# Reordering how three engines build the transform tables at the start of a spectral filter with a GEGLU branch

## The chip, the cores and the metric

The kernel runs on one core of a Trainium2 chip. The metric is the device time of one execution in microseconds (us), here the median of three runs. Profiles come from the hardware profiler and cover one execution each.

## What is computed

A sequence of 2048 rows of width 640 is normalised row by row (xn). One branch takes the real 2-D Fourier transform of xn, multiplies it by complex weights and transforms back. The other is a GEGLU feed-forward net (FFN) on the same xn, with a silu behind it. The product is added to the input.

```python
S, D, F = 2048, 640, 1536
def _A_ref(x, w_r, w_i):                 # spectral branch
    X = jnp.fft.rfft2(x.astype(jnp.float32), axes=(-2, -1))
    X = X * (w_r + 1j * w_i)
    return jnp.fft.irfft2(X, s=(S, D), axes=(-2, -1)).astype(jnp.bfloat16)
def _B_ref(x, w_gate, w_up, w_down):     # FFN branch
    return (_gelu(x @ w_gate) * (x @ w_up)) @ w_down
x = A_x
xn = _layernorm(x, axis=-1)
s = _A_ref(xn, A_w_r, A_w_i)
g = _silu(_B_ref(xn, B_w_gate, B_w_up, B_w_down))
return x + s * g
```

## The kernel before

**Tiling.** The 2048 rows are 16 slabs of 128 rows; slab n1 holds the rows n1, n1+16, n1+32 and so on. Four slabs make a group of the FFN. The transforms are matmuls with tables of sines and cosines that the kernel makes itself: along the rows in two steps (128 points by Tinv and Tfwd, 16 points by MG, N1 and N2), along the width by FT (forward) and FI (inverse).

**Engines.** TensorE (PE) runs all matmuls and transposes. ScalarE (ACT) applies gelu, silu and Sin and copies results out of PSUM. VectorE (DVE) does the row statistics, most of the normalising, the gating product uT, and elementwise work of the spectral branch. GpSimd (POOL) does the roots of the variances and the integer and float phases of the tables. SyncE (SP) issues all DMAs, in one queue. Every engine runs its own instructions strictly in the order in which the program issues them.

**The order** is written out by hand. The list `back` holds 144 pieces of FFN work, called places here: places 0 to 2 are FFN pieces of slabs 0 and 1 with the normalising of slabs 1 to 3; places 3 to 7 are the tiles t = 3 to 7 of the columns of slabs 0 and 1; places 8 to 15 the tiles 0 to 7 of the columns of slabs 2 and 3; places 16 to 23 the tiles 8 to 11 of the whole group 0, psg (gate) and psu (up) in turn; places 24 to 35 the down projection of group 0. Three more groups follow, of 24 pieces and 12 down pieces each. `put(s, f, ...)` lets f be issued right behind place s, in the order of the put lines. Each gate piece issues five matmuls into a bank psg and then a gelu on ACT (L669); each up piece five matmuls into a bank psu and then the product uT on DVE (L671). There are two banks of each kind, so a piece waits until the piece two before it of its kind has been read.

**The tables.** Each of the five columns of the forward table FT starts as an ACT instruction `ft_v` (L328): index times a scale plus a bias, both per partition, from the list `ab`. Three POOL instructions (`ft_phase`, L333, L335, L337) reduce the phases, and `ft_sin` on ACT takes the Sin. Steps 0 to 4 belong to FT, 5 to 9 to FI. Tinv comes from POOL phases (`tinv_phase`, L303), a mask on DVE (`tinv_mask`, L308) in two halves, and a Sin on ACT (L315); `tfwd` transposes it to Tfwd. The 16-point table comes from `mg_iota`, `mg_phase1` and `mg_phase2` (POOL: 2, 11 and 8 small instructions), `mg_mask` (DVE), `mg_sin` (ACT) and `mg_build` (POOL). The scales and biases in `ab` are small DVE constants of one column: `fwd_consts` makes those of the forward table, `inv_consts` those of the inverse table.

**Normalising.** `stats(n1)` takes mean and variance of a slab on DVE. `root(n0, n)` adds eps on DVE (ve, L188) and raises to the power -1/2 on POOL (rst, L190) for n slabs at once. Slabs 0 to 3 have their roots one by one and are normalised on DVE (`norm`, `norm_parts`, L196). Slabs 4 to 7 have one root of four columns and a `shift` (POOL: nm, then nmr, L424), and ACT normalises them (`norm_act`, L429) in places 15, 17, 19 and 21. Their transposes for FFN group 1 are DMA transposes (`slab_T(..., 2)`, L460), put in places 17 to 23 and issued by SP behind the loads that stand ahead of them in its queue. `fold_a` and `fold_b` (DVE) prepare pairs of normalised slabs for the spectral branch; `slab_S1` (PE, then Z on ACT, L478) and `pair_D` (pd) carry them through the first two transforms, and the results go through DRAM (ZDR) to the next stage, `pair_S2` (px).

**Around the change.** Ahead of place 0 the program issues `fwd_consts`, the first half of an iota, stats(0), root(0, 1), `inv_consts`, then warm-up matmuls, norm of slab 0, stats(1), slab 0's transposes, two more warm-ups and root(1, 1).

Of the kernel before, what the change touches and what calls it, by code (L numbers as in the profile page):

```python
# [31 lines left out]
def kernel(  # L32
# [40 lines left out]
    with tc.manual_schedule():  # L73
        build(nc, locals())


def build(nc, env):
# [79 lines left out]
    def c1(name, dt=FP32):  # L157
        return consts.tile([P, 1], dt, name=name)
# [26 lines left out]
    def root(n0, n):  # L185
        m = mva[n0 // 4][:, n0 % 4:n0 % 4 + n, :]
        ve = work.tile([P, 4], FP32, tag="ve", name="ve")[:, 0:n]
        nc.vector.tensor_scalar(out=ve, in0=m[:, :, 1], scalar1=1e-5, scalar2=None, op0=ALU.add)  # L188
        r = work.tile([P, 4], FP32, tag="rst", bufs=4, name="rst")[:, 0:n]
        nc.gpsimd.tensor_tensor(out=r, in0=ve, in1=mhalf[:, 0:n], op=ALU.pow)  # L190
        rall[n0] = r
        for k in range(n):
            rstd[n0 + k] = r[:, k:k + 1]
# [29 lines left out]
    def bits(name, fields):  # L223
        n = len(fields)
        ti = consts.tile([P, n], INT32, name=name + "i")
        tf = consts.tile([P, n], FP32, name=name)
        for k, (shift, mask) in enumerate(fields):
            nc.vector.tensor_scalar(out=ti[:, k:k + 1], in0=pint, scalar1=shift, scalar2=mask,
                                    op0=ALU.logical_shift_right, op1=ALU.bitwise_and)
        nc.vector.tensor_copy(out=tf, in_=ti)  # L230
        return [tf[:, k:k + 1] for k in range(n)]

    def affine(name, src, a, b):
        t = c1(name)
        nc.vector.tensor_scalar(out=t, in0=src, scalar1=float(a), scalar2=float(b), op0=ALU.mult, op1=ALU.add)
        return t

    u_f, hi_f, s_f, h_f, pf, n1_f, z_f = bits(
        "pb", [(0, 63), (6, 1), (0, 31), (5, 1), (0, 127), (1, 15), (0, 1)])
# [4 lines left out]
    def fma(name, src, k, add, dt=FP32):  # L244
        t = c1(name, dt)
        nc.vector.scalar_tensor_tensor(out=t, in0=src, scalar=float(k), in1=add, op0=ALU.mult, op1=ALU.add)
        return t
# [8 lines left out]
    def times(name, src, k, by):  # L256
        t = c1(name)
        nc.vector.scalar_tensor_tensor(out=t, in0=src, scalar=k, in1=by, op0=ALU.mult, op1=ALU.mult)
        return t
# [6 lines left out]
    ab = []  # L266
    kc = []
# [10 lines left out]
        ab.extend([(a_m, b_0), (a_m, b_1), (a_m, b_2), (a_m, b_3), (a_r, b_r)])  # L278

    def inv_consts():  # L280
        cq = kc[0]
        i_0 = affine("i_0", pf, 4.0, 0.0)
        i_1 = affine("i_1", pf, 4.0, 4.0)
        i_2 = affine("i_2", pf, 4.0, 2.0)
        o_0 = affine("o_0", pf, 2.0, 320.0)
        o_1 = affine("o_1", pf, 2.0, 2.0)
        o_2 = affine("o_2", pf, 2.0, 321.0)
        o_3 = affine("o_3", pf, 2.0, 1.0)
        l_k = fma("l_k", h_f, 2.0, affine("l_s", s_f, 2.0, 256.0))
        l_r = fma("l_r", times("lh", affine("hk", h_f, -2.0, 1.0), 1.0, hi_f), 1.0, l_k)  # L290
        i_r = affine("i_r", l_r, 2.0, 0.0)
        o_r = fma("o_r", l_r, 1.0, cq)
        ab.extend([(i_0, o_0), (i_1, o_1), (i_2, o_2), (i_2, o_3), (i_r, o_r)])

    fwd_consts()
    vt_iota(0)
    stats(0)
    root(0, 1)
    inv_consts()

    def tinv_phase(h):
# [201 lines left out]
    def warm_pe(n):  # L503
        if not warm_bank:
            warm_bank.append(bank(0))
        for _ in range(n):
            nc.tensor.matmul(warm_bank[0][:, 0:256], lhsT=ones[:, 0:P], rhs=ones, start=True, stop=True)
# [238 lines left out]
    def put(s, *item):  # L746
        plan[s].append(item)
# [2 lines left out]
    put(5, slab_T, 2, 1)  # L750
    put(6, slab_T, 3, 0)
    for g in range(5):
        put(7 + g, ft_v, g)
        put(12 + g, ft_v, 5 + g)
    put(7, tinv_phase, 0)
    put(7, tinv_phase, 1)
    put(9, mg_iota)
    put(9, mg_phase1)
    for k in range(3):
        put(11, ft_phase, 0, k)  # L760
    for k in range(4):
        put(7 + 2 * k, stats, 4 + k)
    put(13, root, 4, 4)
    put(13, shift, 4, 4)
    put(13, mg_phase2)
    for k in range(3):
        put(16, ft_phase, 1, k)
    put(14, tinv_mask, 0)
    put(15, tinv_mask, 1)
    for k in range(4):  # L770
        put(15 + 2 * k, norm_act, 4 + k)
        put(17 + 2 * k, slab_T, 4 + k, 2)
# [3 lines left out]
    for it in ((silu_table,), (tinv_sin,), (ft_sin, 0)):  # L776
        put(23, *it)
    put(24, fold_b, 0)
    put(25, mg_mask)
    put(25, root, 8, 2)  # L780
    put(25, mg_sin)
    put(25, mg_build)
    put(25, fold_a, 1)
    put(26, tfwd, 0)
    put(27, tfwd, 1)
# [1 line left out]
    put(28, fold_b, 1)  # L787
    put(29, stats, 10)
    put(29, ft_sin, 1)
    put(31, norm, 9)  # L790
    put(32, stats, 11)
    put(33, root, 10, 2)
# [59 lines left out]
    slab_Tparts(0)  # L852
    warm_pe(2)
    root(1, 1)

    put(5, phase_const)

# [35 lines left out]
```

## Time and profile before

| | us |
|---|---|
| median of three runs | 209.15 |
| lowest, highest | 209.08, 209.93 |
| profiled execution | 209.03 |
| its span, first to last instruction | 207.3 |
| PE busy | 198.6 (96%) |
| DVE busy | 132.2 (64%) |
| ACT busy | 124.6 (60%) |
| POOL busy | 34.5 (17%) |

The granted clock of PE was 0.999 of full speed over the span. The page of the profile cuts the span into 40 slices of 5.2 us and gives the busy share of each in tenths (9 is 90% or more):

```profile
PE   7799997999999999999999999999999999999993
POOL 5327799592001100000000000000000000000000
```

PE is below 90% in the first two slices, in the sixth (26 to 31 us) and in the last. POOL has nearly all its work in the first nine slices.

In the chain of waits, each piece of time belongs to the engine that the end of the program waited for at that moment. A timeline row gives start and length in us, engine, line, operation, written tile, read tiles, shapes, how many instructions the row merges, and in brackets the idle time ahead with what ended it. A row's length is from the start of its first instruction to the end of its last. Instructions of one engine overlap somewhat, so the next may start before the last has ended.

### The profile page before, as it was taken

What the parts mean: (1) busy time and instruction counts of PE and PEld (TensorE: products, weight loads), DVE (VectorE), ACT (ScalarE), POOL (GpSimd) and SP (SyncE); (2) the same over time, 40 slices, a digit from 0 to 9 for tenths busy, and PEclk for the clock granted to TensorE, in tenths of its full rate; (3) what the DMA queues carried; (4) which work ended last, traced back from release to release, by engine and by line L of the source; (5) the groups of instructions that cost most, each with busy time, mean ns of one, the idle gap of its engine ahead of it and who ended that gap; (6) DMA issues with size and microseconds to landing.
All of it is one profiled execution on the core that took longest, in us unless ns stands there. A gap on an engine that the chain in (4) does not pass through costs nothing.

```text
span 207.3 us, 4412 instructions
## 1 busy us (share of the span) xinstructions
PE 198.6 (96%) x1626; PEld 121.0 (58%) x1643; DVE 132.2 (64%) x357; ACT 124.6 (60%) x230; POOL 34.5 (17%) x61
## 2 busy tenths in 40 slices
PE   7799997999999999999999999999999999999993
PEld 5689853677655555465544444447775555556762
DVE  7787867896679762335555656424469678676653
ACT  2436729957887777425777777533555555656631
POOL 5327799592001100000000000000000000000000
PEclk9999999999999999999999999999999999999999
DMA  6999999999886999279964432349822332242111
GB/s 175 304 300 310 373 279 145 152 140 129 185 152 164 188 190 183 76 169 224 207 136 96 95 67 63 77 104 294 259 74 87 95 92 101 64 133 76 67 51 65
DMA packets 46200, 31.81 MB, mean 153 GB/s; under 512 B 12513, under 2 KB 43873, under 8 KB 46177
## 3 DMA queue, kind: packets, MB, share of 16 engines
q1 hardware_dynamic: 46176, 31.52, 67.3%
q8 instruction: 13, 0.21, 0.5%
q14 instruction: 11, 0.08, 0.2%
HBM read 21.66 MB, written 7.88 MB: 143 GB/s over the span
## 4 chain that ended last, share of the span: by engine, by line
PE 85%; DVE 5%; POOL 4%; issue 2%; ACT 1%; DMA 1%; DVEq 0%; ACTq 0%
PE psg L665 22%; PE psu L665 22%; PE psg L689 13%; PE psu L689 11%; PE pd L485 4%; PE pu L547 3%; PE pv L592 2%; PE pz L476 2%; PE pd L489 2%; PE px L527 2%; DVE st L174 2%; POOL GEN L335 1%; POOL rst L190 1%; DMA X<-in_A_x_dram 1%; POOL GEN L337 1%
## 5 line engine op out<-in xcount | busy, mean ns | idle before, releaser
L665 PE MATMUL psg<-xnT,Wg 128*128 128x512 bf16 (+2 forms) x284 | 59.9, 338 | 2.1 <-ACT ge L669 1.2
L665 PE MATMUL psu<-xnT,Wu 128*128 128x512 bf16 (+2 forms) x289 | 60.4, 339 | 0.6 <-issue 0.3
L671 DVE TENSOR_TENSOR uT<-psu,ge 128x512 bf16<-128x512 f32 (+2 forms) x59 | 34.4, 587 | 33.9 <-PE psu L665 27.3
L669 ACT ACTIVATE ge<-psg 128x512 bf16<-128x512 f32 (+2 forms) x59 | 30.5, 518 | 28.5 <-PE psg L665 27.3
L689 PEld LDWEIGHTS <-uT 128*128 128x128 bf16 x384 | 36.1, 98 | 15.2 <-issue 0.5
L665 PEld LDWEIGHTS <-Wu 128*128 128x128 bf16 x295 | 26.5, 98 | 21.8 <-issue 1.3
L665 PEld LDWEIGHTS <-Wg 128*128 128x128 bf16 x295 | 26.2, 98 | 22.1 <-issue 2.6
L689 PE MATMUL psg<-Wd,uT 128*128 128x320 bf16 (+1 forms) x192 | 30.4, 303 | 0.0
L689 PE MATMUL psu<-Wd,uT 128*128 128x320 bf16 (+1 forms) x192 | 29.6, 296 | 0.0
L534 DVE TENSOR_TENSOR p<-xs,W 128x642 bf16<-128x642 bf16 x32 | 14.4, 492 | 8.9 <-ACT xs L530 8.5
L497 ACT CAST zd<-pd 128x644 bf16<-128x644 f32 x15 | 12.3, 883 | 4.6 <-PE pd L489 4.6
L606 ACT ACTIVATE eo<-pd 128x640 bf16<-128x640 f32 x16 | 10.4, 701 | 7.4 <-PE pd L489 7.4
L594 ACT CAST vs<-pv 128x640 bf16<-128x640 f32 x16 | 11.0, 690 | 6.1 <-PE pv L592 6.1
L174 DVE BATCH_NORM_STATS2 st<-X 128x6 f32<-128x320 bf16 x32 | 14.1, 482 | 0.2 <-issue 0.2
L530 ACT CAST xs<-px 128x642 bf16<-128x642 f32 x16 | 11.1, 692 | 4.0 <-PE px L527 3.6
L190 POOL TENSOR_TENSOR rst<-ve,mhalf 128x1 f32<-128x1 f32 (+2 forms) x9 | 7.5, 831 | 30.4 <-DVE ve L188 30.4
L615 DVE TENSOR_TENSOR cs<-eo 128x640 bf16<-128x640 bf16 x16 | 7.1, 486 | 7.4 <-ACT eo L606 7.4
L478 ACT CAST Z<-pz 128x640 bf16<-128x640 f32 x16 | 11.0, 696 | 1.2 <-PE pz L476 1.2
L640 DVE TENSOR_TENSOR Yall<-Yall,G 128x640 bf16<-128x640 bf16 (+3 forms) x18 | 8.1, 450 | 1.8 <-ACT G L694 1.6
L698 DVE SCALAR_TENSOR_TENSOR G<-th,psg 128x320 bf16<-128x320 f32 x8 | 3.9, 486 | 7.6 <-ACT th L697 7.6
L641 DVE TENSOR_TENSOR Yall<-Yall,xt 128x640 bf16<-128x640 bf16 (+3 forms) x18 | 8.2, 455 | 0.6
L547 PE MATMUL pu<-p,N 64*64 64x321 bf16 x128 | 8.2, 304 | 0.1
(138 smaller groups left out, 214.8 us busy)
## 6 DMA issues: line engine op xcount, KB each, us to landing
ZDR<-zd SPq DMA_DIRECT2D x16, 160.5 KB, 4.1
UDR<-us SPq DMA_DIRECT2D x32, 80.2 KB, 2.5
xt<-in_A_x_dram SPq DMA_DIRECT2D x8, 320.0 KB, 3.1
W<-in_A_w_r_dram SPq DMA_DIRECT2D x14, 160.5 KB, 7.5
W<-in_A_w_i_dram SPq DMA_DIRECT2D x14, 160.5 KB, 5.0
out_dram<-Yall SPq DMA_DIRECT2D x14, 160.0 KB, 1.8
B<-ZDR SPq DMA_DIRECT2D x6, 321.0 KB, 8.2
Vin<-UDR SPq DMA_DIRECT2D x6, 321.0 KB, 5.5
```

Source lines behind the costliest of these rows:

```text
L174: nc.vector.bn_stats(out=st[:, k, :], in_=X[:, n1, 320 * k:320 * k + 320])
L478: nc.scalar.copy(out=Zt[n1], in_=pz)
L497: ev(out=zd.rearrange("p a c (m b) -> p a c m b", b=2)[:, :, :, :, b], in_=pd[b])
L530: nc.scalar.copy(out=xs.rearrange("p (k l) -> p k l", k=2), in_=px[:, :, 0:L])
L534: nc.vector.tensor_tensor(out=pp, in0=xs, in1=WT[:, h].rearrange("p k l -> p (k l)"), op=ALU.mult)
L547: nc.tensor.matmul(pu[64 * lo:64 * lo + 64, hh, 0:L], lhsT=NM[r, kind, 0:64], rhs=pp[r, lo * L:(lo + 1) * L], start=first, stop=not first)
L594: nc.scalar.copy(out=vs, in_=pv)
L606: nc.scalar.activation(out=eo[:, b], in_=py[b], func=ACT.Copy, scale=(2.0 if n0 // 4 in BY_SILU else 1.0) / (S * D))
L665: nc.tensor.matmul(ps, lhsT=WT[:, c, t * P:(t + 1) * P], rhs=xnT[g][:, c, c0:c1_], start=(c == 0), stop=(c == 4))
L669: nc.scalar.activation(out=ges[t], in_=ps, func=ACT.Gelu_apprx_tanh)
L671: nc.vector.tensor_tensor(out=uT[g][:, t, c0:c1_], in0=ps, in1=ges[t], op=ALU.mult)
L689: nc.tensor.matmul(ph, lhsT=uT[g][:, t, j * P:(j + 1) * P], rhs=Wd[:, t, c0:c1_], start=(t == 0), stop=(t == NT - 1))
```

## The change

Three things are edited, and no arithmetic is added or dropped.

- `inv_consts` is split. Seven constants of the first four inverse columns and the two that need only `s_f` and `h_f` (l_s, hk) stay where they were; the five others (l_k, lh, l_r, i_r, o_r) form `inv_rest`, issued behind root(1, 1).
- The ten ACT steps `ft_v` move from places 7 to 16 to places 3 to 12.
- On POOL, the forward phases (`ft_phase` 0) move from place 11 to 9, and the inverse phases (`ft_phase` 1) from place 16 to 13, behind root and shift of slabs 4 to 7. All phases of the 16-point table move behind those, in place 13; before, its iotas and first phases stood in place 9 and its second ones right behind the shift. On DVE the masks of Tinv move from places 14 and 15 to 12 and 14, and `mg_mask` from 25 to 28; `mg_sin` and `mg_build` move from place 25 to 29, behind `ft_sin` 1.

The queues of PE and SP issue the same instructions in the same order as before. On POOL the forward phases now follow the Tinv phases directly, then come the root of slabs 4 to 7, nm and nmr, the inverse phases and the 16-point phases. On ACT the steps come earlier among the gelus, with the copy of slab 2's transpose now directly ahead of the third step, and mg_sin comes behind the Sin of FI.

```diff
     def inv_consts():
-        cq = kc[0]
         i_0 = affine("i_0", pf, 4.0, 0.0)
...
         o_3 = affine("o_3", pf, 2.0, 1.0)
-        l_k = fma("l_k", h_f, 2.0, affine("l_s", s_f, 2.0, 256.0))
-        l_r = fma("l_r", times("lh", affine("hk", h_f, -2.0, 1.0), 1.0, hi_f), 1.0, l_k)
+        ab.extend([(i_0, o_0), (i_1, o_1), (i_2, o_2), (i_2, o_3)])
+        kc.append(affine("l_s", s_f, 2.0, 256.0))
+        kc.append(affine("hk", h_f, -2.0, 1.0))
+
+    def inv_rest():
+        cq, l_s, hk = kc
+        l_k = fma("l_k", h_f, 2.0, l_s)
+        l_r = fma("l_r", times("lh", hk, 1.0, hi_f), 1.0, l_k)
         i_r = affine("i_r", l_r, 2.0, 0.0)
         o_r = fma("o_r", l_r, 1.0, cq)
-        ab.extend([(i_0, o_0), (i_1, o_1), (i_2, o_2), (i_2, o_3), (i_r, o_r)])
+        ab.append((i_r, o_r))
...
     for g in range(5):
-        put(7 + g, ft_v, g)
-        put(12 + g, ft_v, 5 + g)
+        put(3 + g, ft_v, g)
+        put(8 + g, ft_v, 5 + g)
     put(7, tinv_phase, 0)
     put(7, tinv_phase, 1)
-    put(9, mg_iota)
-    put(9, mg_phase1)
     for k in range(3):
-        put(11, ft_phase, 0, k)
+        put(9, ft_phase, 0, k)
     for k in range(4):
         put(7 + 2 * k, stats, 4 + k)
     put(13, root, 4, 4)
     put(13, shift, 4, 4)
-    put(13, mg_phase2)
     for k in range(3):
-        put(16, ft_phase, 1, k)
-    put(14, tinv_mask, 0)
-    put(15, tinv_mask, 1)
+        put(13, ft_phase, 1, k)
+    for it in (mg_iota, mg_phase1, mg_phase2):
+        put(13, it)
+    put(12, tinv_mask, 0)
+    put(14, tinv_mask, 1)
...
-    put(25, mg_mask)
+    put(28, mg_mask)
     put(25, root, 8, 2)
-    put(25, mg_sin)
-    put(25, mg_build)
     put(25, fold_a, 1)
...
     put(29, ft_sin, 1)
+    put(29, mg_sin)
+    put(29, mg_build)
...
     root(1, 1)
+    inv_rest()
```

## The prediction

> **What bounds the kernel now.** I read the chain of waits first, over the whole span and then for its first 50 us; then the timelines of TensorE (PE), ScalarE (ACT), VectorE (DVE) and GpSimd (POOL) from 3 to 57 us; then the DMA issues that feed PE.
>
> ```profile
> PE 85%; DVE 5%; POOL 4%; issue 2%; ACT 1%; DMA 1%; DVEq 0%; ACTq 0%
> ```
>
> PE holds 85% of the chain. The rest is almost all ahead of 32.3 us, so only there can a change outside PE shorten anything. The chain of waits there (start, length, engine, written tile, line):
>
> ```profile
> 22.19 0.52 ACT GEN L328
> 22.79 0.88 POOL GEN L333
> 23.74 2.95 POOL GEN L335
> 26.76 2.14 POOL GEN L337
> 28.91 1.44 POOL rst L190
> ...
> 31.67 0.58 ACT ge L669
> 32.30 1.24 PE psg L665 x5
> ```
>
> POOL starts the forward table's phases when the fifth table step (L328) is done, needs some 6.1 us for them, and only then takes the root of slabs 4 to 7 (L190). The rows of PE and ACT show what that costs (start, length, operation, in brackets the idle time ahead of it):
>
> ```profile
> 29.86 1.24 PE L665 MATMUL psu<-xnT,Wu 128*128 128x512 bf16 x5
> 32.30 1.24 PE L665 MATMUL psg<-xnT,Wg 128*128 128x512 bf16 x5 [1.19 <-ACT ge L669]
> 30.84 0.92 ACT L429 ACTIVATE X<-X,nmr,rst 128x640 bf16<-128x640 bf16 x1 [3.77 <-POOL nmr L424]
> ```
>
> ACT stands in norm_act(4) until nmr comes at 30.8; the gelu of place 16 is behind it in ACT's queue, and its bank is what place 20 needs. Groups of five such matmuls follow each other 1.08 us apart, so place 20 was ready at 30.94 and started at 32.30: 1.36 us lost. The other stretch not set by PE is the start, on DVE and POOL:
>
> ```profile
> 4.93 0.16 DVE L246 SCALAR_TENSOR_TENSOR l_k<-pb,l_s 128x1 f32<-128x1 f32 x1
> ...
> 5.65 0.15 DVE L246 SCALAR_TENSOR_TENSOR o_r<-l_r,cq 128x1 f32<-128x1 f32 x1
> 5.71 0.63 DVE L196 TENSOR_SCALAR X<-X,mva,rst 128x384 bf16<-128x384 bf16 x2
> ...
> 8.25 0.64 DVE L196 TENSOR_SCALAR X<-X,mva,rst 128x384 bf16<-128x384 bf16 x2 [0.68 <-POOL rst L190]
> ```
>
> Slab 0's root was done at 5.08 (POOL row 4.50, 0.58 long), but its norm waited in DVE's queue behind the dependent constants until 5.71.
>
> **The change, part by part.** *Inverse constants split.* Eight constants and then hk stay ahead of norm(0); hk would issue near 4.81 instead of 5.01. Norm(0) then waits for the root alone: 5.08 plus the 0.03 that L196 took after the root at 8.22, so 5.11 against 5.71: 0.60 us earlier. Stats(1) follow at 5.65; their slab landed 3.9 us after its issue at 1.64, near 5.55, just in time. The five moved operations (l_k to o_r) stand behind ve of slab 1, where DVE idled 0.68 us for the root: with the spacings of before (0.07 for a free one, 0.19 to 0.20 for one that waits for the last) they take 6.88 to 7.48, and norm(1) is released by its root at 7.64. Cost nothing; without that cover 0.6. From there to place 5 the chain is DVE, POOL and PE work that moves along (the weights of places 3 to 7 land 1.4 us or more ahead of use). Bounds of this part: 0 (slab 1 late) to 0.60; I take 0.60, as every row on the way moves with it.
>
> *Forward table steps in places 3 to 7.* Ten ACT steps move four places earlier, none is added. At places 3, 4, 6, 7 and later they fill ACT's waits for PE (0.3 to 0.9 us; a step occupies the queue 0.42). At place 5 the step stands between the copy of slab 2's transpose and the gelu of place 6, which was back to back (15.63, 16.22): the gelu is 0.42 later, uT of place 6 some 0.28, as it waited for PE until 0.08 after the gelu, and so is the copy of slab 3's transpose (17.13 to 17.61) that place 8's matmul at 17.89 needs. Loss 0.05 us, between 0 and 0.3.
>
> *POOL's order.* All later times carry the 0.55 gained so far. POOL has the two phases of the 2048-point table (2.37 us) from 15.9 to 18.2, then the forward phases at once, since the fifth table step is done at 17.7: 0.87, 2.94 and 1.61 (L337's length the second time), with the 0.08 between them, to 23.8. The 4.5 us of the 16-point table's iotas, phase1 and phase2 on both sides of the root go behind it. On DVE, tinv_mask(0) now stands ahead of stats(7), in place 12. The two masks of before show what happens when one meets POOL:
>
> ```profile
> 26.63 0.81 DVE L308 TENSOR_SCALAR GEN<-GEN,andm,orm 128x1024 int32<-128x1024 int32 x1
> 27.68 1.77 DVE L308 TENSOR_SCALAR GEN<-GEN,andm,orm 128x1024 int32<-128x1024 int32 x1
> ```
>
> L337 ran from 26.76 to 28.90. The first mask started ahead of it and was free, and L337 took 2.14 instead of 1.61; the second started inside it, ended 0.55 after it, and took 0.96 more. So each waits for the other's end. In the new order mask 0 begins at 23.7, at L337's end, and waits 0.2 us at most; the uT of place 13 and stats(7) behind it run some 0.3 later than they would (24.71 and 25.05 before, less 0.55, plus 0.3), and ve ends near 26.1. The root of four columns took 1.48 with mask 1 inside it until 29.45, so 0.9 alone; 128x1 takes 0.56 and 128x2 alone 0.72 (row at 64.83), which extrapolates to 1.06. I take 1.06, up to 1.48: root 26.2 to 27.3. Mask 1, in place 14, starts inside the root and ends 0.55 after it, at 27.8; nm waits for that, nmr is ready at 28.3 (28.7 with the long root). Behind mask 1, uT of place 15 ends near 28.2, and the bank it frees is wanted by place 19 at 29.3. Free.
>
> Norm_act(4) starts at 28.3, the gelu of place 16 0.83 later, done at 29.7; place 20 wants its bank at 30.38. The stall is gone with 0.65 to spare: gain 1.36, between 0.7 (nmr 1.3 late) and 1.36. Norm_act(5) to (7) lie ahead of gelus that wait for PE. The Sin table load then starts 2.1 us earlier than before, Tinv is done at 37.8, and PE comes to its transposes at 37.95: another 0.12 (before, they started at 39.99 though PE was free at 39.87).
>
> *16-point table.* POOL's phases for the inverse table now run 28.3 to 33.9, phase1 and phase2 to 39.6 or, if fold_a and fold_b (two-input bf16 operations on DVE, 2.8 us of them) always win, 42.4. Then root(8,2), norm(8) near 41 to 43, the mask of vg, and ACT's Sin of it behind FI at 43.4. Z(0) may start as late as 44.2 before PE's pd waits. Cost nothing, bounds 0 to 0.3. Mg_build follows to 48, root(10,2) at 47.2 to 48.8 with 1.05 us of idle DVE time behind norm(10). SP's queue keeps its order and no DMA is moved.
>
> *Sum:* 0.60 - 0.05 + 1.36 + 0.12 = 2.03. Against it stands what comes next: slabs 4 to 7 reach the second FFN group by DMA transposes, issued in SP's queue behind loads whose pace is set by earlier landings. The last of them, and the matmul that needs it:
>
> ```profile
> L460 SPq DMA_TRANSPOSE xnT<-X x1: 1598/1598/1598, 47.6 to 47.6; - x1
> ...
> DMA to landing us min/median/max: 4.0/4.0/4.0
> ```
>
> ```profile
> 53.64 1.25 PE L665 MATMUL psg<-xnT,Wg 128*128 128x512 bf16 x4
> ```
>
> It lands at 51.6 whatever PE does, so of any gain only 53.64 - 51.64 = 2.0 us gets past this point. Later, from 94 us, the ZDR loads have 2.2 us of slack at the second px (row 95.87; its data landed at 89.45 + 4.2) and follow compute anyway. So 2.0 us off the profiled 209.03 (span 207.3, 1.73 around it): 207.03, span 205.3. The median of the three runs is 0.12 above the profiled one: 207.15, given as 207.1.
>
> **A rule against the split.** L_k started inside slab 0's root (4.50 to 5.08) and took 0.16, as l_r did outside it, so I let l_r run inside slab 1's root. The Trainium skill, page "SBUF — State Buffer", section "Who interferes with whom", says that a VectorE instruction with two SBUF inputs and a GpSimd instruction that reads SBUF exclude each other for the whole instruction. By that, l_r would wait from 7.13 to 7.61 and the first part would shrink.
>
> **Rivals.** (1) The part at the start shrinks: l_r is held by the root until 7.61, norm(1) follows 0.33 later (5.38 to 5.71 before), 0.31 earlier instead of 0.60. Sum 1.74, 207.4. For: the masks' rows; against: l_k's row. 0.10. (2) Nothing of the start reaches PE, because slab 1 lands late or place 8 eats it: 1.36 + 0.12, 207.7. 0.09. (3) The stall becomes a DMA wait: the transposes land a us later than before, or nmr comes 1.3 late; the gain is 0.5 to 1.0, 208.4. For: 2.0 us of slack is all there is; against: the DMA order is untouched. 0.15. (4) Slower: POOL's backlog. If the small phase operations and DVE's folds hold each other up, mask and Sin of vg come late, and ACT, in order, holds Z(0) and Z(1) behind them. From 43.85 on each us of delay is a us of PE; slower by 1.2 needs 43.85 + 2.0 + 1.2 = 47.1, phase2 ending some 6 us after 39.6. For: an L349 of 0.29 took 1.44 at 43.08 beside DVE work; against: only 2.8 us of such work is there. 210.4. 0.06.
>
> **Numbers.** The forecast has 0.60: 207.1, itself 206.7 to 207.4. With rivals 1 and 2 it holds 0.79, so the range is 206.6 to 208.1. About 0.5% (1.05 us) is what can be told from no change: faster 0.79, same 0.15, slower 0.06.
>
> **What would show it.** PE's 1.19 us wait for ge gone and norm_act(4) at 28 to 29 us; norm(0) at 5.1 and norm(1) at 7.6 (7.9 for rival 1); the four-column root ahead of mask 1's end; psg of the second group near 51.65, right behind the last transpose. Wrong, if PE waits for ACT's ge or Z between 28 and 50, or if the transposes land after 52.5.

## The result, and the profile after

The changed kernel takes 207.09 us (median of 6 runs, 207.05 to 208.18) against 209.11 us before in the same measurement (6 runs, 208.97 to 209.93): ratio 0.9907, 95% interval 0.9882 to 0.9932. The profiled execution took 207.12 us with a span of 205.3 us, against 209.03 and 207.3: 1.91 us less, where the prediction's sum was 2.0. Several kernels here have some runs about 1 us longer than the rest (209.93 before and 208.18 after; in a later measurement of the kernel before, 8 of 25 at 209.81 to 210.11); none of these was profiled, and their cause is open. The page of the changed kernel, the busy shares, PE in 40 slices and the chain that ended last by engine (source lines of the changed file stand five below those of before from the edit of the constants on; experiments that leave the constants whole keep the old numbers):

```profile
PE 198.7 (97%) x1626; PEld 121.2 (59%) x1643; DVE 129.9 (63%) x357; ACT 124.7 (61%) x230; POOL 33.9 (17%) x61
PE   7999999999999999999999999999999999999993
PE 90%; DVE 4%; DMA 2%; issue 1%; ACT 1%; POOL 1%; SPq 0%; DVEq 0%
```

PE has gone from 85% of the chain to 90%, POOL from 4% to 1%. Two slices of PE have filled up, the second and the seventh. (The stall ahead of place 20, at 31 to 32.3 us, lies in the seventh slice of the kernel before, which is 31 to 36 us, and not in the sixth, as stated above.) PE's waits in the first 60 us say which ones went (line waited at, releaser, us in all, times, longest; a wait of 1.2 us of the warm-up matmuls is the same in both). Before:

```profile
PE psg L665 <- ACT ge L669: 1.2, 1, 1.2
PE pt L724 <- DVE X L196: 1.0, 2, 0.7
```

After:

```profile
PE pt L729 <- DVE X L196: 0.3, 1, 0.3
```

The wait for the gelu is gone and the wait for the normalised slabs at the start is 0.7 us shorter (two waits among others, so their sum is not the gain). Place 20, in the timelines of PE and ACT of the changed kernel (start, length, operation, idle time ahead in brackets):

```profile
29.43 1.24 PE L670 MATMUL psu<-xnT,Wu 128*128 128x512 bf16 x5
30.51 1.24 PE L670 MATMUL psg<-xnT,Wg 128*128 128x512 bf16 x5
27.76 0.92 ACT L434 ACTIVATE X<-X,nmr,rst 128x640 bf16<-128x640 bf16 x1 [1.53 <-POOL nmr L429]
28.59 0.57 ACT L674 ACTIVATE ge<-psg 128x512 bf16<-128x512 f32 x1
```

Place 20 follows place 19 at the usual 1.08 us, at 30.51 instead of 32.30. Of the 1.79 us, 0.44 were there already at place 8 (17.45 instead of 17.89); the other 1.35 are the stall. What released it, in the timelines of POOL and DVE:

```profile
22.32 1.62 POOL L342 TENSOR_TENSOR GEN<-GEN 128x805 f32<-128x805 f32 x1
23.77 0.81 DVE L313 TENSOR_SCALAR GEN<-GEN,andm,orm 128x1024 int32<-128x1024 int32 x1
25.98 0.17 DVE L188 TENSOR_SCALAR ve<-mva 128x4 f32<-128x4 f32 x1
26.23 1.04 POOL L190 TENSOR_TENSOR rst<-ve,mhalf 128x4 f32<-128x4 f32 x1 [2.29 <-DVE ve L188]
26.40 0.81 DVE L313 TENSOR_SCALAR GEN<-GEN,andm,orm 128x1024 int32<-128x1024 int32 x1
27.24 0.20 POOL L354 TENSOR_SCALAR nm<-mva 128x4 f32<-128x4 f32 x1
27.52 0.20 POOL L429 TENSOR_TENSOR nmr<-nm,rst 128x4 f32<-128x4 f32 x1
```

POOL now waits 2.29 us for ve, and ACT's wait for nmr is 1.53 us instead of 3.77, short enough for the gelu to be in time. Mask 1 starts 0.17 us behind the root and runs its 0.81 inside it, held by nothing. The start, on DVE and POOL:

```profile
5.02 0.64 DVE L196 TENSOR_SCALAR X<-X,mva,rst 128x384 bf16<-128x384 bf16 x2 [0.16 <-POOL rst L190]
5.78 0.89 DVE L174 BATCH_NORM_STATS2 st<-X 128x6 f32<-128x320 bf16 x2
7.18 0.57 POOL L190 TENSOR_TENSOR rst<-ve,mhalf 128x1 f32<-128x1 f32 x1 [2.20 <-DVE ve L188]
7.27 0.16 DVE L246 SCALAR_TENSOR_TENSOR l_r<-lh,l_k 128x1 f32<-128x1 f32 x1
7.78 0.63 DVE L196 TENSOR_SCALAR X<-X,mva,rst 128x384 bf16<-128x384 bf16 x2
```

Norm(0) waits for the root alone. It is 0.69 us earlier, and 0.09 of that is not the change's: slab 0 itself landed at 2.98 us instead of 3.07. L_r runs its 0.16 us inside slab 1's root. Stats(1) start at 5.78 instead of 6.26 and norm(1) at 7.78 instead of 8.25: 0.47 us, not 0.60. The last transpose of slabs 4 to 7 and the matmul that needs it, in the view of tile xnT (two transposes, the last issued at 47.5; the shortest landing is its) and PE's timeline:

```profile
L465 SPq DMA_TRANSPOSE xnT<-X x2: 1227/1741/2255, 45.2 to 47.5; - x2
DMA to landing us min/median/max: 3.3/3.8/4.2
51.73 1.25 PE L670 MATMUL psg<-xnT,Wg 128*128 128x512 bf16 x4
```

It landed at 47.55 + 3.28 = 50.83, 0.9 us ahead of its use. And the 16-point table, on POOL and ACT:

```profile
40.37 0.73 POOL L190 TENSOR_TENSOR rst<-ve,mhalf 128x2 f32<-128x2 f32 x1
43.54 0.39 ACT L397 ACTIVATE sg<-vg,negpi 128x128 f32<-128x128 int32 x1
43.83 0.68 ACT L483 CAST Z<-pz 128x640 bf16<-128x640 f32 x1
```

Phase2 ends at 40.4 where the root starts; the Sin of vg comes right behind FI's on ACT, and Z(0) at 43.83.

### The profile page after: what moved, and what is told of

Its sections match the earlier page's. It is cut to its first block, busy times and chain, and to the rows that moved or that the text cites. A ratio compares the mean times of both kernels' runs of the same rounds, so it can differ in the third digit from the quotient of the medians.

```text
span 205.3 us, 4412 instructions
## 1 busy us (share of the span) xinstructions
PE 198.7 (97%) x1626; PEld 121.2 (59%) x1643; DVE 129.9 (63%) x357; ACT 124.7 (61%) x230; POOL 33.9 (17%) x61
## 4 chain that ended last, share of the span: by engine, by line
PE 90%; DVE 4%; DMA 2%; issue 1%; ACT 1%; POOL 1%; SPq 0%; DVEq 0%
PE psu L670 24%; PE psg L670 24%; PE psg L694 13%; PE psu L694 12%; PE pd L490 5%; PE pu L552 3%; PE pv L597 2%; PE pz L481 2%; DMA X<-in_A_x_dram 2%; PE pd L494 2%; PE px L532 2%; DVE st L174 1%; DVE uT L676 1%; POOL rst L190 1%; PE pt L326 0%
## 5 line engine op out<-in xcount | busy, mean ns | idle before, releaser
L190 POOL TENSOR_TENSOR rst<-ve,mhalf 128x1 f32<-128x1 f32 (+2 forms) x9 | 6.5, 719 | 27.2 <-DVE ve L188 27.2
```

## Experiments

Each run is read by its time and by the start of the second FFN group on PE (psg 53.64 before, 51.73 after): in all traces but one the time is 155.4 to 155.5 us more than that start, so nothing behind it differs. The exception is the run of the steps alone, with 155.8.

### One part at a time

**The split alone**, in the kernel before (the `inv_consts`, `inv_rest` and call of the change's diff, nothing else).

> The kernel before with only the split of the inverse constants. Theory (the start is a chain that moves everything behind it): norm(0) at 5.0 to 5.1 us, stats(1) as soon as slab 1 has landed (5.6 to 5.8), psu of place 5 about 0.48 us earlier than 14.61, and since the fifth table step follows PE, the stall ahead of place 20 stays 1.36 long and only moves: 208.6 us. Rival (the stall ahead of place 20 swallows what comes ahead of it): 209.1. Second rival (l_r is held by slab 1's root): 208.8, with l_r longer than 0.16.

Measured: 208.60 us (12 runs, 208.38 to 208.84), ratio 0.9964, interval 0.995 to 0.9978; second group at 53.19, 0.45 earlier. Place 20 of this kernel still stalls:

```profile
31.84 1.24 PE L670 MATMUL psg<-xnT,Wg 128*128 128x512 bf16 x5 [1.19 <-ACT ge L674]
```

The 0.45 us of the start arrive whole at the second group, and the stall is a matter of the other parts.

**All but the split** (the changed kernel with the constants whole).

> The changed kernel with the inverse constants whole again, ahead of norm(0). Theory (the two parts add up): 1.36 + 0.11 - 0.04 of gain is left, 207.6 us, and no wait of PE for ge between 28 and 33 us. Rival (the split is needed so that the gelus come in time): PE waits for ge again and the time is 208.3 or more.

Measured: 207.63 us (6 runs, 207.53 to 208.64), ratio 0.9931, interval 0.9909 to 0.9953; second group at 52.16, 1.48 earlier, without a stall at place 20. 0.45 + 1.48 = 1.93 against the 1.91 of both: the parts add. (0.05 of the 1.48 come from an earlier slab 0, as the table further down shows.)

**The ACT steps alone**, in the kernel before.

```diff
-        put(7 + g, ft_v, g)
-        put(12 + g, ft_v, 5 + g)
+        put(3 + g, ft_v, g)
+        put(8 + g, ft_v, 5 + g)
```

> The kernel before with only the ten ACT table steps moved four places ahead; POOL's and DVE's order stays, so the forward phases follow mg_phase1, at 21.8 instead of 22.8. Theory (root waits for POOL's queue, and the queue for the fifth step; one us of POOL time is enough to take most of the stall away): forward phases end near 27.4, ve of slabs 4 to 7 is held by the last of them until then, root 27.5 to 28.6, nmr 29.0 to 29.5, and place 20 starts within 0.3 us of PE being ready: 207.7 to 208.1. Rival (only the new order on POOL takes the stall away): 208.9 to 209.2.

Measured: 208.04 us (8 runs, 207.89 to 208.86), ratio 0.9953, interval 0.9935 to 0.9971; second group at 52.26, 1.38 earlier. POOL and DVE in this kernel:

```profile
25.77 1.61 POOL L337 TENSOR_TENSOR GEN<-GEN 128x805 f32<-128x805 f32 x1
26.27 1.13 DVE L188 TENSOR_SCALAR ve<-mva 128x4 f32<-128x4 f32 x1
27.48 1.03 POOL L190 TENSOR_TENSOR rst<-ve,mhalf 128x4 f32<-128x4 f32 x1
```

With the 16-point phases still ahead of them, the forward phases end at 27.38 and ve ends with them, so the root starts 1.25 us later than after the whole change. It is nearly in time all the same: place 20 loses about 0.03 us. In time the gain is less, 0.99 us in the profiled run and 1.03 in the median: 0.28 is lost again near 109 us, where one matmul group of the spectral branch (pu) starts 0.39 us behind the group ahead of it (px) instead of 0.16 as in the kernel before, and 0.09 lies outside the profiled span. Why it is lost is not known.

**The order of POOL and DVE alone** (the kernel before with the 16-point phases right behind the shift, and with the masks, `mg_mask`, `mg_sin` and `mg_build` where the change puts them; the steps and the forward and inverse phases stay where they were).

```diff
-    put(9, mg_iota)
-    put(9, mg_phase1)
...
-    put(13, mg_phase2)
...
-    put(14, tinv_mask, 0)
-    put(15, tinv_mask, 1)
+    for it in (mg_iota, mg_phase1, mg_phase2):
+        put(13, it)
+    put(12, tinv_mask, 0)
+    put(14, tinv_mask, 1)
```

> The changed orders on POOL and DVE (16-point phases behind the shift, masks in places 12 and 14, mask, Sin and build of the 16-point table later), but the table steps in places 7 to 16 as before, the forward phases in place 11, the inverse ones in place 16, and the constants whole. Theory (the fifth step sets the forward phases): they start at 22.8 as before, mask 0 of place 12 comes at 24.2, inside L335's turn on POOL, and waits for its end near 26.7; the product of place 13 is then late for place 15; nmr at 30 or later: no gain, 209.0 to 209.6. Rival (POOL's order takes the stall away): 207.6.

Measured: 208.96 us median (12 runs, six at 208.42 to 208.69 and six at 209.23 to 209.75), ratio 0.9988, interval 0.997 to 1.0006; the profiled run took 208.43, second group at 53.03. Without the early steps POOL waits for the fifth of them until 22.70, and 0.83 us of the stall stay. So the steps are what frees POOL; the order alone gives 0.61 us at the second group of the profiled run, 0.09 of it from an earlier slab 0, and 0.11 in the median, which the interval does not tell from nothing. The steps alone give most of the same (1.38 + 0.61 is more than the 1.48 of both). One expectation was wrong, and it is about who holds whom (POOL and DVE):

```profile
23.66 2.94 POOL L335 TENSOR_SCALAR GEN<-GEN 128x805 f32<-128x805 f32 x1
24.11 0.95 DVE L308 TENSOR_SCALAR GEN<-GEN,andm,orm 128x1024 int32<-128x1024 int32 x1
26.68 1.61 POOL L337 TENSOR_TENSOR GEN<-GEN 128x805 f32<-128x805 f32 x1
26.89 1.96 DVE L308 TENSOR_SCALAR GEN<-GEN,andm,orm 128x1024 int32<-128x1024 int32 x1
28.25 1.48 POOL L190 TENSOR_TENSOR rst<-ve,mhalf 128x4 f32<-128x4 f32 x1
```

Mask 0 ran inside L335 at 0.95, not held. Mask 1 started inside L337, waited for its end at 28.29 and ended 0.56 after it, as in the kernel before; and the root, started behind the mask, ended 0.88 after the mask's end.

### Root and mask

**Mask 1 right behind ve**, ahead of the uT of place 14, in the changed kernel.

```diff
     put(13, shift, 4, 4)
+    put(13, tinv_mask, 1)
...
-    put(14, tinv_mask, 1)
```

> The changed kernel with mask 1 issued right behind ve of slabs 4 to 7 (place 13), ahead of place 14's product, so that the mask starts before the root instead of after it. Theory (of mask and root, the one that starts second waits only if the mask is first, as in the kernel before, where the root of 1.48 ended 0.89 after the mask): root 1.4 to 1.6 us long, ending 0.9 after the mask; nmr near 28.2. Rival (mask and root never hold each other up, and the root before was long for another reason): root 1.04. Second rival (whichever is first holds the other, and the mask inside the root of the changed kernel was luck): root as in the theory, but the mask of the other kernels of this call would be 1.3 or longer where it starts inside the root. Time 207.1 with each, as the gelu of place 16 has 0.9 us to spare.

Measured: 206.92 us (one run, too few for a verdict; the trace is what counts here). DVE and POOL:

```profile
25.85 0.81 DVE L313 TENSOR_SCALAR GEN<-GEN,andm,orm 128x1024 int32<-128x1024 int32 x1
26.02 1.53 POOL L190 TENSOR_TENSOR rst<-ve,mhalf 128x4 f32<-128x4 f32 x1 [2.29 <-DVE ve L188]
```

With the mask first the root takes 1.53 and ends 0.89 after the mask's end at 26.66; with the root first (the changed kernel) it takes 1.04 and the mask its 0.81. Between these two only the root is ever held in these traces, and only by a mask that started ahead of it. The run of the steps alone agrees: mask 0 ran inside the root at 0.80, and nmr, started on POOL at 28.78 behind mask 1 (28.70, 0.80 long), took 0.78 instead of 0.20.

### The cover of the 16-point table

**Its second phases written twice, and three times** (`* 3`), in the changed kernel (the same values again).

```diff
     def mg_phase2():
...
-        for ri in range(2):
+        for ri in tuple(range(2)) * 2:
```

> The changed kernel, but the loop of phase2 that writes the eight phases of the 16-point table runs twice over the same values: eight more GpSimd instructions of 0.33 to 0.37 us, some 2.7 us, ahead of the root of slabs 8 and 9. Theory (the 16-point table is free because phase2's end at 40.4 us lies some 3 us ahead of where it counts): phase2 ends at 43.1, the root of slabs 8 and 9 at 43.9, the mask of vg and ScalarE's Sin of it come at 44.4 to 44.6 instead of 43.5, Z(0) a little under 1 us later than its 43.83; 0.4 to 0.5 of that is covered, TensorE loses 0 to 0.5: 207.1 to 207.6. Rival (phase2's end already sets the pace): 2.7 us more, 209.8.

> As the run with the phases written twice, but three times: sixteen more GpSimd instructions, some 5.4 us. Theory (rival 4's mechanism, from 43.85 on each us is a us of TensorE): phase2 ends at 45.8, the Sin of vg at 47.2, Z(0) 3.6 us later, TensorE waits for its pd some 3.1 us: 210.2, slower than before. Rival (VectorE and ScalarE have other work to do first, or the waiting is made up for at the second FFN group, where the last transpose lands at 50.8): 207.1 to 208.

Measured: twice 207.34 us (4 runs, 207.23 to 207.59), ratio 0.9894, interval 0.9866 to 0.9922; phase2 ends at 42.93, sg at 44.37, Z(0) at 44.68, and PE's pd behind it takes 0.92 us instead of 0.74: 0.18 lost, 0.11 of it left at the second group (51.84). Three times 211.70 us (4 runs, 211.54 to 211.76), ratio 1.0099, interval 1.0071 to 1.0127; phase2 ends at 45.65, sg at 47.09, Z(0) at 47.40. PE of the kernel with three:

```profile
48.13 0.32 PE L490 MATMUL pd<-FT,Z 128*128 128x161 bf16 x2 [1.91 <-ACT Z L483]
49.05 0.59 PE L490 MATMUL pd<-FT,Z 128*128 128x161 bf16 x6 [0.60 <-ACT Z L483]
```

And PE by windows of 1 us in the same kernel (window, length, busy time and instructions, granted clock, DMA share, GB/s):

```profile
50.00:51.00 1.00, 1.00 (x7) 0.65 0.00 0
51.00:52.00 1.00, 1.00 (x8) 0.50 0.00 0
52.00:53.00 1.00, 1.00 (x7) 0.50 0.48 145
53.00:54.00 1.00, 1.00 (x7) 0.64 0.81 225
```

The first 2.6 us of delay were almost free, the next 2.7 cost 4.40 at the second group (56.24 against 51.84): 2.51 of waiting for Z, and a halved clock behind it, 0.35 + 0.50 + 0.50 + 0.36 = 1.71 us of lost work; 0.18 is in neither. All four runs of this kernel show the clock: their mean is 0.991 to 0.992, where no run of any other kernel is below 0.996. The expectation had the mechanism and the lateness of Z(0) (3.57 us) right and the wait a little too long (3.1), but knew nothing of the clock; it is 1.5 us short.

### What sets the last 0.5 us

**Slab 1's load ahead of the first gate weights**, in the changed kernel.

```diff
-    load_w(0, 0, 3)
     load_x(1, 1)
+    load_w(0, 0, 3)
```

> The changed kernel with slab 1's load issued ahead of the first three tiles of Wg. Theory (stats(1) wait for slab 1's landing at 5.76, not for DVE): slab 1 lands near 4.5, stats(1) follow norm(0) directly at 5.57 instead of 5.78, and everything behind is 0.2 us earlier: 206.9 us. Rival (Wg then comes late for the first gate matmul at 6.5, or the start is set elsewhere): 207.1 or more.

Measured: 207.15 us (4 runs, 206.92 to 207.63), ratio 0.9913, interval 0.9901 to 0.9926. Slab 1 landed at 3.59 instead of 5.76 and place 5 came 0.15 earlier, not the 0.20 that stats(1) gained. The likely reason is the gate weights, which now landed at 6.59, after PE could have begun on them (6.52 in the changed kernel). In the profiled run (207.63) the last transpose landed at 52.12 and PE waited for it:

```profile
52.16 1.04 PE L670 MATMUL psg<-xnT,Wg 128*128 128x512 bf16 x3 [0.51 <-DMA xnT<-X]
```

The cap of the prediction exists, but not at a fixed time.

**Slab 3's statistics and root one place later** (behind place 3 instead of ahead of it), in the changed kernel, and **both together**.

```diff
-            (run, (ffn_slab, 1, ((1, 1), (2, 1))), (norm, 2), (stats, 3), (root, 3, 1))]
+            (run, (ffn_slab, 1, ((1, 1), (2, 1))), (norm, 2))]
...
+    put(3, stats, 3)
+    put(3, root, 3, 1)
```

> The changed kernel with stats(3) and root(3, 1) issued behind place 3 instead of ahead of it. Theory (psu of place 5 waits at 14.13 for the product of place 3, which stands behind stats(3) in DVE's queue; 0.30 us of PE): the product of place 3 ends near 12.9 instead of 14.1, psu of place 5 starts at 13.83, norm(3) still comes by 15.4: 206.8 us. Rival (slab 3's later root delays its transpose and place 8 gives the gain back): 207.1.

> Both of these edits on the changed kernel. Theory (they add up, and the second FFN group still finds its transposes landed): 206.6 us, psg of the second group near 51.2. Rival (the landing of slab 7's transpose, 50.8 to 52.1 us in the five profiles so far, now sets the start of the second group): that psg starts right at the landing, with a wait of PE ahead of it, and the time stays at 206.8 to 207.4.

Measured: the first 206.79 us (4 runs, 206.61 to 206.97), ratio 0.9896, interval 0.9881 to 0.991; both 207.23 us (6 runs, 206.69 to 207.76), ratio 0.9914, interval 0.9899 to 0.9929. In the first, PE's 0.30 us wait at place 5 (for the uT behind those statistics on DVE) is gone. With both, the second group (51.38) started right behind the last transpose (51.33).

**Weight loads behind the transposes.** The last four groups of the spectral weight loads in SP's queue moved from places 12 to 15 to places 24 to 27, and the edge scaling that waits for them from place 40 to 48: once in the kernel with both edits, once in the one with the statistics alone.

```diff
-        put(8 + k if k < 8 else (32, 35, 38, 41, 44, 44, 47, 47)[k - 8], w_rows, k // 8, k % 8 // 4, k % 2, k % 4 // 2)
-    put(40, w_edge, 0)
+        put((8, 9, 10, 11, 24, 25, 26, 27)[k] if k < 8 else (32, 35, 38, 41, 44, 44, 47, 47)[k - 8], w_rows, k // 8, k % 8 // 4, k % 2, k % 4 // 2)
+    put(48, w_edge, 0)
```

> The kernel with both slab 1's load ahead of Wg and stats(3) behind place 3 (207.23 median, runs from 206.69 to 207.76), with the last four of the eight groups of spectral weight loads in SyncE's queue moved from places 12 to 15 to places 24 to 27, behind the transposes of slabs 4 to 7, and the edge scaling that waits for them from place 40 to 48. Theory (the landing of the last transpose sets the second FFN group in the runs above 207): the transposes are issued from about 36 to 42 us, the last lands by 47 instead of 51.3, TensorE starts the second group behind the work ahead of it at 51.2, and all runs lie near 206.6 with a spread under 0.3. Rival (the spread of the runs has another cause): the median and the spread stay, some runs above 207.2. A second way it could fail: the moved loads delay the transposes of slabs 8 to 11 or the ZDR stores behind them, TensorE waits after 55 us, 207.5 or more.

> The kernel with stats(3) behind place 3 (206.79 median), with the same four groups of loads moved behind the transposes of slabs 4 to 7, and slab 1's load where it was. Theory: there the second group started at 51.22 with the last landing at 50.80, 0.4 us ahead, so TensorE gains nothing on the usual run and 206.6 to 206.8 is expected. Rival: as in the run before, the moved loads make the transposes of slabs 8 to 11 late, 207.3 or more.

Measured: 207.20 us (6 runs, 206.88 to 207.40), ratio 0.9882, interval 0.9856 to 0.9907, and 207.01 us (6 runs, 206.80 to 207.30), ratio 0.9877, interval 0.9854 to 0.99 (beside them the kernel before took 209.02 to 210.16, with a median of 209.24, so these ratios and those of the two kernels with more phases lie below the quotients of the medians). The transposes did land early, the last at 45.20 and 41.70, and neither kernel is faster for it: the landing of the transposes is at most part of the spread (six runs each: 206.69 to 207.76 with both edits, 206.88 to 207.40 with the loads moved as well). PE of the first at its start, and of the second group:

```profile
7.08 0.73 PE L670 MATMUL psg<-xnT,Wg 128*128 128x128 bf16 x10 [0.73 <-DMA Wg<-in_B_w_gate_dram]
51.90 1.25 PE L670 MATMUL psg<-xnT,Wg 128*128 128x512 bf16 x4
```

PE started on the first gate weights at 7.08, when they landed; in the kernel this one was made from (profiled at 206.78) they landed at 6.18 and PE started at 6.61. That is 0.47 of the 0.52 us between the second groups of the two. The second of the two kernels had its late load in slab 1; its stats(1), beside those of the kernel without the moved loads (206.61 profiled):

```profile
5.98 0.89 DVE L174 BATCH_NORM_STATS2 st<-X 128x6 f32<-128x320 bf16 x2 [0.20 <-DMA X<-in_A_x_dram]
```

```profile
5.56 0.88 DVE L174 BATCH_NORM_STATS2 st<-X 128x6 f32<-128x320 bf16 x2
```

Both loads are issued at 1.64 us; one took 4.3, the other 3.8. The start of stats(1), which in the kernel before is

```profile
6.26 0.88 DVE L174 BATCH_NORM_STATS2 st<-X 128x6 f32<-128x320 bf16 x2
```

against the second group's start, in every trace where slab 1's load kept its place, but for the two with more phases:

| kernel | slab 1 landed, us | stats(1) started, us | second group, us | from stats(1) to it | profiled time, us |
|---|---|---|---|---|---|
| before | 5.57 | 6.26 | 53.64 | 47.38 | 209.03 |
| split alone | 5.78 | 5.80 | 53.19 | 47.39 | 208.60 |
| order alone | 5.83 | 6.17 | 53.03 | 46.86 | 208.43 |
| steps alone | 5.74 | 6.28 | 52.26 | 45.98 | 208.04 |
| changed, constants whole | 5.60 | 6.21 | 52.16 | 45.95 | 207.55 |
| changed | 5.76 | 5.78 | 51.73 | 45.95 | 207.12 |
| changed, mask 1 behind ve | 5.57 | 5.59 | 51.53 | 45.94 | 206.92 |
| statistics of slab 3 later | 5.45 | 5.56 | 51.22 | 45.66 | 206.61 |
| the same, weight loads later | 5.96 | 5.98 | 51.65 | 45.67 | 207.12 |

The two parts of the change separate cleanly here. The split moves stats(1) and nothing behind it (47.38 and 47.39); steps and order together take 1.43 us out of what follows, whatever the start. With the split, stats(1) begin when slab 1 has landed or when norm(0) is through, whichever is later: in the changed kernel, the split alone and the last row they start 0.02 us behind the landing, in the other two 0.55 behind the start of norm(0). Norm(0) in turn follows slab 0, which landed between 2.93 and 3.19 us in the traces. The edit of slab 3's statistics is worth 0.28 us counted from stats(1), less than the start varies. The two kernels with it in the table have medians of 206.79 and 207.01, but their intervals overlap the changed kernel's, so a version that beats it is seen in the traces and not told apart in the times.

## Why the prediction held, step by step

- *Inverse constants split, 0.60.* Mechanism right, size off: 0.48 at place 5 (14.13 instead of 14.61), 0.45 alone in its own run. The prediction took slab 1's landing near 5.55 as "just in time"; it landed at 5.76, and stats(1) waited for it until 5.78 instead of 5.65. Landings in the kernels whose first loads keep their order lie between 5.45 and 5.96, so 0.60 was near the best case of a term that a load decides.
- *L_r inside the root.* As taken: 0.16 us at 7.27, in the root's 7.18 to 7.75. The Trainium skill, page "SBUF — State Buffer", section "Who interferes with whom", would have held it until the root's end; this trace does not agree. Rival 1 (207.4) falls by this row.
- *Steps in places 3 to 7, loss 0.05.* 0.48 at place 5, 0.44 at place 8: 0.04.
- *The order, gain 1.36.* 1.35. "Mask 1, in place 14, starts inside the root and ends 0.55 after it, at 27.8; nm waits for that, nmr ready at 28.3" is the step that failed: the mask was done at 27.21 and nmr at 27.72. It came from L337's rows, and L337 is not the root: the root holds no mask, as the changed kernel and the run of the steps alone show. The error lay on the safe side, under 0.65 us of slack. Likewise mask 0's wait of up to 0.2 was none, and ve ended at 26.15 (26.1 predicted), the root at 27.27 (27.3).
- *Tinv, 0.12.* 0.11: tfwd at 38.09 instead of 39.99, 1.90 in all.
- *16-point table, nothing.* Right, with phase2 at 40.4 between the two ends of 39.6 and 42.4. "Z(0) may start as late as 44.2" was a little early: at 44.68 PE lost 0.18, not 0.48. Rival 4 has its mechanism shown by the kernel with three sets: phase2 6 us behind 39.6 is slower than before, but by 2.5 us instead of 1.2 (211.70 against 209.24), since the prediction counted only waiting (3.2 us, of which 2.51 came) and not the clock behind it.
- *The cap, "It lands at 51.6 whatever PE does".* Wrong as a fixed number: the last transpose landed between 50.4 and 52.1 in the kernels with SP's order unchanged, at 50.83 after the change. In the kernels with both parts of the change it was 50.4 to 50.8, in the others, and where slab 1's load stood first, 51.3 to 52.1; why is open. So the second group did not start "right behind the last transpose" but 0.9 us behind it. The sum was cut from 2.03 to 2.0 by it, which cost the forecast nothing; in the run with slab 1 first, where it landed at 52.12, it took 0.51 us. Rival 3 is thus real in other runs, not in this one.
- *Rival 2* (nothing of the start reaches PE, 207.7) falls by the run without the split, whose second group starts 0.43 us later than the changed kernel's.

So of 2.03 the start gave 0.12 too little, and the other terms came within 0.02 each: 1.91. Counted from the start of stats(1), all that follows gave 47.38 - 45.95 = 1.43 us, just what the prediction's other three terms add up to. Open: why the same load takes 3.8 or 4.3 us; and by what rule DVE is held: ve ended with L337 in the run of the steps alone, and with L335 in the kernel before (0.49 long, to 26.70 against 26.68), while mask 0 ran inside L335.

## What to carry to other kernels

When an engine's in-order queue stalls the bound one, look for what could be issued earlier in the queue that feeds it: moving ten ACT steps four places gave 1.38 of the 1.48 us that steps and order gave together at the second group (in time 1.0 of 1.5), and reordering the waiting engine without them gave 0.6 at best. A term that ends "just in time" at a load is worth its range, not its best value: here the landings of two loads moved the whole kernel by 0.4 us. When work is put behind cover, measure the cover by doubling the work: 2.6 us more were almost free, 5.3 us cost more than the wait.

## What the runs showed of the hardware

- Two short waits of PE were followed by a halved clock. Waits of 1.91 and 0.60 us between 46.2 and 49.1 were followed by a granted clock of 0.5 for 1.71 / 0.5 = 3.4 us; a single wait of 1.19 us in the kernel before was not (1.00 in all windows around it). One kernel shows this; what the condition is was not tested. The Trainium skill, page "TensorE: Matmul & The Clock Gate", section "Part 1: The HAM clock gate", gives about 3.4 us as the window over which activity is judged; the length of the slow stretch agrees, while no idle stretch here was as long as such a window.
- Who holds whom between DVE and POOL depended on the pair and the order: a 128x1024 int32 mask was held to L337's end (1.96 and 1.77 us instead of 0.81), ran inside L335 at 0.95 and inside the four-column root at 0.81; the root took 1.48 to 1.53 instead of 1.04 when a mask had started ahead of it. No rule that fits all of these was found.
- DMA transposes issued at the same point of SP's queue landed up to 1.7 us apart from kernel to kernel (50.4 to 52.1).
